# Attention with two feed-forward layers on one core: every full key tile enters the values' product as float32, v comes in one load and a copy, and the maxima's halves are joined ahead of the transpose

## The chip, the core and the metric

The kernel runs on one core of a Trainium2 chip. The time is the device time of one execution in microseconds (us). The kernel before takes 1217.23 us in the median of three runs (1215.57 to 1217.28).

## What is computed

The reference, cut to what matters (4 batches, 8 heads, 576 positions, 64 columns a head; 2304 tokens, 512 columns):

```python
q_rot, k_rot = rotate(q), rotate(k)
scores = (q_rot @ k_rot.T) / sqrt(64)
scores = scores - max(scores, axis=-1)
attn = exp(scores)
attn = attn / (sum(attn, axis=-1) + 1e-09)
x = attn @ v                                   # heads put side by side
x = (sigmoid(x @ w_gate) * (x @ w_val)) @ w_out
h = x @ w_in2
out = where(h > 0, h, exp(min(h, 0)) - 1) @ w_out2
```

## The kernel before

Two stages follow each other. The first is attention over 32 heads (16 pairs), the second is two feed-forward layers over chunks of their weights. The change touches the first alone.

**Tiles.** The 576 keys of a head are four full tiles of 128 and a tail of 64; the 576 queries are two halves of 288. A float32 number x is often held as two parts, a rounded one (hi, type float32r) and the rest (lo = x - hi), so that three float32r products, or fewer, stand for one float32 product.

**Slots and steps.** The program is written out slot by slot, one slot for a head, ten steps in a slot. In step h of slot i, `scores` (L433) issues two matmuls `s` (L459) for tile h // 2 and query half h % 2 of head i, and ScalarE (ACT) takes the exponential; `maxima` (L404) issues one matmul `mt` (L409) for head i + 2, whose negated row maximum VectorE (DVE) takes (L412); `values` (L475) adds one key tile of head i - 1 to its output in PSUM. TensorE (PE) therefore runs s, s, mt and the values' product in every step. Scores use three PSUM banks in turn, the maxima's matmuls three, the values' two.

**An agenda.** Everything else stands in a table, `at(slot, step, function)`: it is issued after the matmuls of that step, and with a half step ahead of the next one's. [...]

- `split_v` (L388): for tiles 0 to 2 of a pair, ACT casts v to a rounded part (VS, L393) and GpSimd (POOL) subtracts (L394); for the tail, L399 and L400 do the same into VT. The agenda has them at steps 1 and 5 of the pair's first slot.
- `scores` for tiles 0 to 2: ACT takes the exponential twice, once into float32 `e` (L462) and once rounded into `ph` (L464); `low_part` (L468) subtracts into `pl` (L471), on DVE for tiles 0 and 2 and the tail, on POOL for tile 1.
- `values` for tiles 0 to 2: three float32r matmuls (L497 to L499). Tile 3 goes as float32: one matmul (L494) of `e` with VF, which the trace shows as two. The tail takes two float32r matmuls (L491, L492).
- Heads 30 and 31 (`LF`, L375) take all five tiles as float32 out of `last_v`.
- `max_all` (L416) joins the two query-half columns of a head's maxima, `max_row` (L420) transposes them on PE (`mr`, L422), ACT copies the row (L424), and a DMA `W<-row` (L426) puts it into the head's operand buffer W, where the head's first scores need it one slot later.
- `rope_ops` (L286) rotates k, q and the tails of a later pair, on POOL in all but the first pair; `split` (L316) transposes them on PE into one of the scores' PSUM banks and makes hi and lo; `move` (L344) copies them into W with three DMAs (`W<-hl`, L358 to L360).
- `inverse` (L519) sends the sums through DRAM and back (`d<-SUM`, `r<-d`, `d<-r`, `rb<-d`), and POOL multiplies (`normalized`, L539).

**Queue.** Every DMA is issued by SyncE (SP), in the order of the agenda. For one pair that is: loads of k and q two pairs ahead (step 0 of an even slot) and of their tails in every other even slot (step 0), the rows (step 1.5 of every slot), the moves (steps 1 and 9 of an odd slot), the sums, v for four heads as three loads of one tile each (step 6 of slots 3, 7, ...), its tails, and VF (step 1 of an odd slot), 256 bytes a row.

**End of the stage.** From slot 29, step 4, the first chunk of the weights is split on DVE, seven instructions for a piece (L124 to L137), between the attention's last steps.

Of the kernel before, what the change touches and what calls it, by code (L numbers as in the profile page):

```python
# [19 lines left out]
def attention_moe_moe_kernel(  # L20
# [40 lines left out]
    NS, NF = len(SP), len(FP)  # L61
# [108 lines left out]
    with ExitStack() as att:  # L170
# [3 lines left out]
        p_p = att.enter_context(tc.tile_pool(name="p", bufs=2 * NS))  # L174
# [39 lines left out]
        def tiles_of_v(b, h, n, t):  # L214
            return v[b, h : h + n, 0:SM, :].rearrange("h (p t) d -> p h t d", t=ST)[:, :, t]

        def load_vf(pr):
            for n in range(NF):
                nc.sync.dma_start(out=VF[pr % 2][:, :, n, 0:D], in_=tiles_of_v(*divmod(2 * pr, H), 2, FP[n]))

# [29 lines left out]
        VF = [const.tile([P, 2, NF, 2 * D], F32, name=f"VF{par}") for par in range(2)]  # L250
        VS = [const.tile([P, 2, NS, 3 * D], F32R, name=f"VS{par}") for par in range(2)]
# [15 lines left out]
        def constants_v(par):  # L267
            nc.gpsimd.memset(VF[par][:, :, :, D : 2 * D], 1.0)
            nc.gpsimd.memset(VS[par][:, :, :, 2 * D : 3 * D].bitcast(F32), 1.0)
# [16 lines left out]
        def rope_ops(pr, which, eng):  # L286


            hd = D // 2
# [26 lines left out]
        def split(pr, which, half):  # L316

            if (pr, which) == (pr, "k") and half == 0:
                if pr == 1:

                    parts[pr] = [p_p.tile([P, S], F32R, tag=tag, name=f"hl1_{n}") for n, tag in enumerate(("ph", "pl", "ph", "pl"))]
                else:
                    parts[pr] = hl_p.tile([P, 4, S], F32R, tag="hl", name=f"hl{pr}")
# [96 lines left out]
        def max_row(i):  # L420
# [7 lines left out]
                in_=row.bitcast(F32),  # L428
            )

        probs = {}

        def scores(i, h):  # L433

# [404 lines left out]
```

## Time and profile before

| | |
|---|---|
| median of three runs | 1217.23 us |
| the profiled execution | 1214.78 us, its span 1213.0 us |
| PE | 1163.2 us busy (96%) |
| DVE | 995.6 us (82%) |
| POOL | 689.2 us (57%) |
| ACT | 499.4 us (41%) |
| mean granted TensorE clock | 0.990 |

Busy time is what an engine spent in instructions; matmuls are pipelined, so that a busy PE need not be a full one. What a change in one stage is worth is read from that stage alone: the attention's heads, its end, and the feed-forward layers have different limits. A wait is put down to what came last of the things waited for.

### The profile page before, as it was taken

The page shows a single profiled execution, that of the slowest core. Times are in us where ns is not written, and L with a number is a line of the kernel's source. Part 1 is how long each engine was busy: PE and PEld are TensorE (multiplying, and loading weights), DVE is VectorE, ACT ScalarE, POOL GpSimd, SP SyncE. Part 2 cuts the span into 40 slices and gives each one's busy share as a digit, 9 for nine tenths or more (in the row PEclk, how much of TensorE's full clock was granted, in tenths as well). Part 3 has the DMA queues.
Part 4 walks back from the last instruction along what each step waited for, and adds up shares of the span by engine and source line. Part 5 has one row for each costly group of instructions (what it writes and reads, how often), then busy time and mean ns, then how long its engine had stood idle before and what let it go on. Part 6 is the DMA issues. An engine that isn't in the chain of part 4 may idle for free.

```text
span 1213.0 us, 17583 instructions
## 1 busy us (share of the span) xinstructions
PE 1163.2 (96%) x5956; PEld 983.2 (81%) x5956; DVE 995.6 (82%) x2024; ACT 499.4 (41%) x1251; POOL 689.2 (57%) x731
## 2 busy tenths in 40 slices
PE   5898999999889999999999999999999999999998
PEld 4787888887857888888888888888888887888887
DVE  8888887887798987867777676778999999999844
ACT  3777777877744532122222222344422222222221
POOL 8977888887355555443444344666554545545421
PEclk9999999999999999999999999999999999999999
DMA  7676666755523121111111111101111111110004
GB/s 186 138 154 140 137 151 140 158 131 128 137 73 97 36 70 53 51 37 36 53 39 49 52 36 35 35 20 51 53 35 53 35 52 36 53 36 18 1 35 122
DMA packets 71146, 89.53 MB, mean 74 GB/s; under 512 B 35920, under 2 KB 44400, under 8 KB 71056
## 3 DMA queue, kind: packets, MB, share of 16 engines
q1 hardware_dynamic: 71056, 88.41, 28.4%
q8 instruction: 47, 0.77, 0.3%
q14 instruction: 43, 0.35, 0.1%
HBM read 56.01 MB, written 4.87 MB: 50 GB/s over the span
## 4 chain that ended last, share of the span: by engine, by line
PE 58%; DVE 9%; ACT 1%; issue 0%
PE h L680 12%; PE h L681 12%; PE h L682 12%; PE o L680 8%; PE o L681 8%; PE o L682 8%; DVE z L763 2%; DVE g L706 1%; DVE g L705 1%; DVE ca L130 1%; DVE cm L137 1%; DVE cm L127 1%; DVE ce L124 1%; DVE ce L133 1%; DVE cm L125 1%
## 5 line engine op out<-in xcount | busy, mean ns | idle before, releaser
L712 POOL TENSOR_TENSOR gl<-g,gh 128x512 fp32r<-128x512 f32 (+1 forms) x140 | 168.6, 1204 | 326.2 <-ACT gh L711 260.4
L711 ACT CAST gh<-g 128x512 fp32r<-128x512 f32 (+1 forms) x140 | 81.2, 580 | 306.6 <-DVE g L706 172.0
L459 PE MATMUL s<-W 128*128 128x288 f32 (+1 forms) x640 | 164.2, 339 | 22.9 <-DMA W<-row 9.6
L680 PE MATMUL h<-xh,wh 128*128 128x512 f32 (+1 forms) x480 | 177.3, 369 | 1.7 <-ACT xh L665 1.3
L681 PE MATMUL h<-xl,wh 128*128 128x512 f32 (+1 forms) x480 | 177.5, 370 | 1.0 <-DVE xl L666 1.0
L682 PE MATMUL h<-xh,wl 128*128 128x512 f32 (+1 forms) x480 | 177.1, 369 | 0.0
L138 POOL TENSOR_TENSOR ca<-ca,wh 128x256 f32<-128x256 f32 x136 | 113.8, 837 | 94.6 <-DVE cm L134 89.0
L412 DVE TENSOR_REDUCE MX<-mt 128x1 f32<-128x288 f32 (+1 forms) x320 | 132.6, 444 | 23.4 <-PE mt L409 22.0
L462 ACT ACTIVATE e<-s 128x288 f32<-128x288 f32 (+1 forms) x320 | 127.7, 411 | 50.1 <-PE s L459 10.8
L135 ACT CAST wh<-ca 128x256 fp32r<-128x256 f32 x136 | 55.3, 407 | 215.9 <-DVE ca L130 215.9
L459 PEld LDWEIGHTS s<-W 128*128 128x128 f32 (+1 forms) x640 | 101.1, 185 | 48.2 <-ACT ph L464 13.8
L140 POOL TENSOR_TENSOR wl<-ca,cm 128x256 fp32r<-128x256 f32 x136 | 113.0, 831 | 18.5 <-DVE cm L137 11.4
L681 PE MATMUL h<-yl,wh 128*128 128x512 f32 (+1 forms) x320 | 117.7, 368 | 0.0
L682 PE MATMUL h<-yh,wl 128*128 128x512 f32 (+1 forms) x320 | 117.7, 368 | 0.0
L680 PE MATMUL h<-yh,wh 128*128 128x512 f32 (+1 forms) x320 | 117.7, 368 | 0.0
L680 PE MATMUL o<-wh,gh 128*128 128x512 f32 x288 | 112.8, 392 | 1.6 <-DVE z L763 1.2
L681 PE MATMUL o<-wl,gh 128*128 128x512 f32 x288 | 112.2, 390 | 0.0
L682 PE MATMUL o<-wh,gl 128*128 128x512 f32 x288 | 112.1, 389 | 0.0
L701 DVE TENSOR_TENSOR g<-h,g 128x512 f32<-128x512 f32 (+1 forms) x60 | 38.2, 637 | 88.6 <-PE h L682 85.8
L409 PE MATMUL mt<-W 128*128 128x288 f32 (+1 forms) x320 | 100.5, 322 | 7.5 <-DVE MX L412 4.5
L680 PEld LDWEIGHTS h<-xh,wh 128*128 128x128 f32 x480 | 90.9, 189 | 17.9 <-ACT xh L665 1.7
L681 PEld LDWEIGHTS h<-xl,wh 128*128 128x128 f32 x480 | 90.8, 189 | 16.4 <-DVE xl L666 1.5
(116 smaller groups left out, 2875.2 us busy)
## 6 DMA issues: line engine op xcount, KB each, us to landing
W<-hl SPq DMA_DIRECT2D x89, 288.0 KB
raw<-in_moe_w_out_dram SPq DMA_DIRECT2D x28, 512.0 KB
raw<-in_moe_w_in_dram SPq DMA_DIRECT2D x16, 512.0 KB
raw<-in_moe_w_gate_dram SPq DMA_DIRECT2D x12, 512.0 KB
raw<-in_moe_w_val_dram SPq DMA_DIRECT2D x12, 512.0 KB
rb<-d SPq DMA_DIRECT2D x32, 144.0 KB
k<-in_k_dram SPq DMA_DIRECT2D x16, 256.0 KB
q<-in_q_dram SPq DMA_DIRECT2D x16, 256.0 KB
```

The costliest lines, as they stand in the source:

```text
L135: nc.scalar.copy(h, a)
L138: nc.gpsimd.tensor_tensor(out=a, in0=a, in1=h.bitcast(F32), op=ALU.subtract)
L140: nc.gpsimd.tensor_tensor(out=l, in0=a, in1=mf, op=ALU.add)
L409: nc.tensor.matmul(m[0:n, 0:HS], lhsT=operand(i, "Q1", t * P, n), rhs=operand(i, "K1", a * HS, HS), start=True, stop=True)
L412: nc.vector.tensor_reduce(out=MX[i % 3][0:n, a, t : t + 1], in_=m[0:n, 0:HS], axis=AX.X, op=ALU.max, negate=True)
L459: nc.tensor.matmul(s, lhsT=operand(i, st, t * P, n), rhs=operand(i, mv, a * HS, HS), start=st == "K1", stop=st == "K2")
L462: nc.scalar.activation(e[:, c], s, AF.Exp)
L680: nc.tensor.matmul(ps, lhsT=ah, rhs=bh, start=j == 0, stop=False)
L681: nc.tensor.matmul(ps, lhsT=ah, rhs=bl, start=False, stop=False)
L682: nc.tensor.matmul(ps, lhsT=al, rhs=bh, start=False, stop=j == n - 1)
L711: nc.scalar.copy(hi, g)
L712: nc.gpsimd.tensor_tensor(out=lo, in0=g, in1=hi.bitcast(F32), op=ALU.subtract)
```

## The change

All four full key tiles go the way of tile 3 before: one exponential into float32 `e`, no rounded part and no low part, one float32 matmul with VF. VF holds all four tiles; v comes in one load of 1 KB pieces for four heads, and POOL copies it into VF, two slots after the load. VS, `load_vf`, `load_last` and the special way of heads 30 and 31 are gone; those two heads now take the tail's way of the others. `max_all` stands at step 0.5, ahead of `max_row` at 1.5 (before: at 2, behind it, so that the row held the first half's maxima alone). The rotation is three instructions instead of four. Pair 1 is moved with three DMAs for each head as the other pairs are. Loads of k and q go from step 0 to 3, tails from 0 to 4, v from slot 4g - 1, step 6 to slot 4g - 2, step 8, the first move of a pair from step 11 to 12, and `split_v` from steps 1 and 5 to 5 and 7. PSUM tiles keep one bank each.

```diff
-    KINDS = ("vector","gpsimd","vector",None)
-    FP = [t for t, kind in enumerate(KINDS) if kind is None]
-    SP = [t for t, kind in enumerate(KINDS) if kind is not None]
...
-        p_p = att.enter_context(tc.tile_pool(name="p", bufs=2 * NS))
+        p_p = att.enter_context(tc.tile_pool(name="p", bufs=2))
...
         def load_v(g):
-            b, h = divmod(4 * g, H)
-            t = raws["v", g] = v_p.tile([P, 4, NS, D], F32, tag="v", name=f"v{g}")
-            for n in range(NS):
-                nc.sync.dma_start(out=t[:, :, n], in_=tiles_of_v(b, h, 4, SP[n]))
+            load("v", 4 * g, 4, v_p)
             load_tails("vv", g, v_p)
...
-        VF = [const.tile([P, 2, NF, 2 * D], F32, name=f"VF{par}") for par in range(2)]
-        VS = [const.tile([P, 2, NS, 3 * D], F32R, name=f"VS{par}") for par in range(2)]
+        VF = [const.tile([P, 2, ST, 2 * D], F32, name=f"VF{par}") for par in range(2)]
...
-            for a in range(2):
-                lo, hi = slice(a * hd, (a + 1) * hd), slice((1 - a) * hd, (2 - a) * hd)
-                tt(out=sv[..., lo], in0=x[..., hi], in1=sin[..., lo], op=ALU.mult)
-                yield
+            axes = "p n" if which == "t" else "p h t"
+            two = lambda y: y.rearrange(f"{axes} (two d) -> {axes} two d", two=2)
+            tt(out=two(sv), in0=two(x)[..., ::-1, :], in1=two(sin), op=ALU.mult)
+            yield
...
             if piece == 0:
-                vs = VS[par]
-                nc.scalar.copy(vs[..., D : 2 * D], x)
-                nc.gpsimd.tensor_tensor(
-                    out=vs[..., 0:D], in0=x, in1=vs[..., D : 2 * D].bitcast(F32), op=ALU.subtract
-                )
+                nc.gpsimd.tensor_copy(VF[par][..., 0:D], x)
...
+                if t == ST:
+                    tail[i] = e_p.tile([P, S], F32, tag="e", name=f"e{i}_{t}")[TL:P]
+                    probs[i, t] = p_p.tile([P, S], F32R, tag="pt", name=f"pt{i}")
                 else:
+                    probs[i, t] = e_p.tile([P, S], F32, tag="ef", name=f"e{i}_{t}", bufs=2 * ST)
...
             nc.scalar.activation(e[:, c], s, AF.Exp)
-            if hi is not None:
-                nc.scalar.activation(hi[:, c], s, AF.Exp)
+            if t == ST:
+                nc.scalar.activation(probs[i, t][TL:P, c], s, AF.Exp)
...
-            elif hi is None:
-                nc.tensor.matmul(out_ps, lhsT=VF[par][:, ab, FP.index(t)], rhs=e[:, c], start=t == 0, stop=False)
-            else:
-                vs = VS[par][:, ab, SP.index(t)]
-                nc.tensor.matmul(out_ps, lhsT=vs[:, D : 3 * D], rhs=lo[:, c], start=t == 0, stop=False)
-                nc.tensor.matmul(out_ps[0:D], lhsT=vs[:, 0:D], rhs=hi[:, c], start=False, stop=False)
-                nc.tensor.matmul(out_ps, lhsT=vs[:, D : 3 * D], rhs=hi[:, c], start=False, stop=False)
+            else:
+                nc.tensor.matmul(out_ps, lhsT=VF[par][:, ab, t], rhs=e, start=t == 0, stop=False)
...
-            at(*((i - 2, 9) if i == 0 else (i - 1, 2)), max_all, i)
+            at(*((i - 2, 9) if i == 0 else (i - 1, 0.5)), max_all, i)
...
-                at(s0 - 4, 15 if pr == 2 else 11, move, pr, 0)
+                at(s0 - 4, 15 if pr == 2 else 12, move, pr, 0)
                 at(s0 - 4, 19, move, pr, 1)
             for piece in range(2 if pr > 0 else 0):
-                at(s0, (1, 5)[piece], split_v, pr, piece)
-            if pr > 1:
-                at(s0 - 1, 1, load_vf, pr)
+                at(s0, (5, 7)[piece], split_v, pr, piece)
         for pr in range(2, NPAIR):
-            slot, step = {3: (-1, 9), 4: (1, 0)}.get(pr, (2 * pr - 8, 0))
+            slot, step = {3: (-1, 9), 4: (1, 3)}.get(pr, (2 * pr - 8, 3))
...
-            at(*((1, 0) if g == 2 else (4 * g - 8, 0)), load_tails, "qk", g, raw_p)
-            at(4 * g - 1, 6, load_v, g)
+            at(*((1, 4) if g == 2 else (4 * g - 8, 4)), load_tails, "qk", g, raw_p)
+            at(4 * g - 2, 8, load_v, g)
...
-        at(*(29, 0), load_last)
```

On SP, the DMAs from slot 19 to slot 20 stood like this before (r8, d2_8 and rb8 are the sums of pair 8, W11 is the operand buffer of head 23, v5 and vv5 are v for heads 20 to 23, k28, q28 and qk7 the loads of a later pair, and row21 is the row of head 21):

```order
L530 DMA r8_3551<-d2_8_3550 128x9
L211 DMA v5_3626<-in_v_dram 128x4x64 x3
L202 DMA vv5_3630<-in_v_dram 64x4x64 x2
L358 DMA W11_158<-hl11_3438 64x1152
L359 DMA W11_158<-hl11_3438 64x2x576
L360 DMA W11_158<-hl11_3438 64x1152
L533 DMA d2_8_3550<-r8_3551 128x9
L192 DMA k28_3687<-in_k_dram 128x2x256
L192 DMA q28_3689<-in_q_dram 128x2x256
L202 DMA qk7_3691<-in_q_dram 64x4x64
L202 DMA qk7_3691<-in_k_dram 64x4x64
L426 DMA W01_156<-row21_3714 1x5x128
```

and now, from v for the same heads on:

```order
L186 DMA v20_2906<-in_v_dram 128x4x256
L196 DMA vv5_2908<-in_v_dram 64x4x64 x2
L451 DMA d2_8_2964<-SUM_88 2x576
L372 DMA W00_153<-row20_2969 1x5x128
L322 DMA W10_155<-hl11_2863 64x1152
L323 DMA W10_155<-hl11_2863 64x2x576
L324 DMA W10_155<-hl11_2863 64x1152
L453 DMA r8_2965<-d2_8_2964 128x9
L322 DMA W11_156<-hl11_2863 64x1152
L323 DMA W11_156<-hl11_2863 64x2x576
L324 DMA W11_156<-hl11_2863 64x1152
L456 DMA d2_8_2964<-r8_2965 128x9
```

Row 21 is the next DMA behind these, and k28 and q28 stand behind it. So between the sums and the row of head 21 the loads of v, of k and q and of their tails are gone, and the row of head 20 and the sums stand ahead of a pair's first move, which they followed before.

On ACT, the first steps of slot 28 stood like this before (e28 and ph28 are the two exponentials, VS0 the rounded v of heads 28 and 29, v7 its load):

```order
L462 ACTIVATE e28_0_4984<-s28_1_5001 128x288
L464 ACTIVATE ph28_0_4985<-s28_1_5001 128x288
L393 CAST VS0_161<-v7_4939 128x6x64
L424 CAST row29_5016<-mr29_5014 5x128
L462 ACTIVATE e28_1_5019<-s28_2_5022 128x288
L464 ACTIVATE ph28_1_5020<-s28_2_5022 128x288
```

and now:

```order
L397 ACTIVATE e28_0_4136<-s28_0_4137 128x288
L397 ACTIVATE e28_0_4136<-s28_1_4149 128x288
L370 CAST row29_4159<-mr29_4157 5x128
L397 ACTIVATE e28_1_4162<-s28_2_4163 128x288
L397 ACTIVATE e28_1_4162<-s28_3_4171 128x288
```

The second exponential of each step and the cast that reads v7 have left ACT; the copy that reads v7 now stands on POOL.

On DVE, at the turn from slot 18 to slot 19 (mt20_9 is the last matmul of head 20's maxima, MX2 where they stand, pt18 the tail's low part), it was:

```order
L412 TENSOR_REDUCE MX2_167<-mt20_9_3496 64x1
L412 TENSOR_REDUCE MX0_165<-mt21_0_3517 128x1
L513 COPY u8_3269<-pv17_1_3431 64x288
L342 TENSOR_TENSOR hl11_3438<-Tq11_256_3525,hl11_3438 128x320
L471 TENSOR_TENSOR pt18_3474<-e18_4_3473,pt18_3474 64x576
L412 TENSOR_REDUCE MX0_165<-mt21_1_3537 128x1
L412 TENSOR_REDUCE MX0_165<-mt21_2_3566 128x1
L418 TENSOR_TENSOR MX2_167<-MX2_167 128x5
L471 TENSOR_TENSOR pl19_0_3511<-e19_0_3509,ph19_0_3510 128x576
```

and it is now:

```order
L358 TENSOR_REDUCE MX2_163<-mt20_9_2922 64x1
L358 TENSOR_REDUCE MX0_161<-mt21_0_2939 128x1
L437 COPY u8_2729<-pv17_1_2859 64x288
L364 TENSOR_TENSOR MX2_163<-MX2_163 128x5
L314 TENSOR_TENSOR hl11_2863<-Tq11_256_2946,hl11_2863 128x320
L404 TENSOR_TENSOR pt18_2896<-e18_4_2895,pt18_2896 64x576
L358 TENSOR_REDUCE MX0_161<-mt21_1_2957 128x1
L358 TENSOR_REDUCE MX0_161<-mt21_2_2977 128x1
```

The join of the halves has moved up four places, and PE's transpose mr20, two steps into the slot, now needs it; the low part pl19 is gone.

## Rows read from the trace of the kernel before

**Rows 1.** Stages: us, busy PE, PEld, DVE, ACT, POOL, clock, DMA share, GB/s.

```profile
25.90:65.80 39.90, 36.44 (x231) 31.48 (x230) 34.51 (x71) 30.83 (x95) 37.20 (x39) 1.00 0.60 134
65.80:246.80 181.00, 167.94 (x1061) 146.74 (x1059) 147.61 (x318) 138.99 (x414) 149.37 (x154) 0.96 0.66 146
246.80:328.20 81.40, 74.52 (x488) 66.61 (x486) 66.07 (x145) 62.34 (x187) 53.51 (x54) 0.98 0.61 141
328.20:366.00 37.80, 30.37 (x155) 23.02 (x152) 36.67 (x81) 20.91 (x60) 22.39 (x25) 0.95 0.23 63
366.00:1213.00 847.00, 840.30 (x3983) 705.76 (x3983) 688.99 (x1364) 238.81 (x486) 405.13 (x420) 1.00 0.15 46
```

**Rows 2.** The same stretches, transposes mr of the maxima alone, one a head.

```profile
25.90:65.80 39.90, 1.23 (x4) 0.35 (x4) 1.00 (x4) 1.00 0.60 134
65.80:246.80 181.00, 5.07 (x17) 1.59 (x17) 4.32 (x17) 0.96 0.66 146
246.80:328.20 81.40, 2.17 (x8) 0.69 (x8) 2.03 (x8) 0.98 0.61 141
```

**Rows 3.** Timeline of PE, two maxima transposes: start, us, engine, line, operation, tiles.

```profile
246.84 0.27 PE L422 MATMUL mr<-ident,MX 128*5 128x128 f32 x1
...
254.81 0.27 PE L422 MATMUL mr<-ident,MX 128*5 128x128 f32 x1
```

**Rows 4.** Timeline of PE, two steps of slot 19, and transposes of slot 18.

```profile
216.69 0.38 PE L330 MATMUL Tk<-ident,rk 128*128 128x128 f32 x2
216.96 0.54 PE L459 MATMUL s<-W 128*128 128x288 f32 x2
...
219.03 0.38 PE L330 MATMUL Tk<-ident,rk 128*128 128x128 f32 x2
...
219.54 0.47 PE L459 MATMUL s<-W 128*64 128x288 f32 x2
...
224.17 0.29 PE L409 MATMUL mt<-W 128*128 128x288 f32 x1
...
224.96 0.30 PE L409 MATMUL mt<-W 128*128 128x288 f32 x1
225.10 0.65 PE L494 MATMUL pv<-e,VF 128*128 128x288 f32 x2
...
225.85 0.29 PE L409 MATMUL mt<-W 128*128 128x288 f32 x1
```

**Rows 5.** Timeline of SP, from a pair's first move to head 21's row.

```profile
223.59 0.49 SPq L358 DMA_DIRECT2D W<-hl  x1
...
230.38 1.48 SPq L211 DMA_DIRECT2D v<-in_v_dram  x3
...
237.27 1.29 SPq L192 DMA_DIRECT2D k<-in_k_dram  x1
...
240.56 0.77 SPq L426 DMA_DIRECT2D W<-row  x1
```

**Rows 6.** Timeline of PE, the first scores of slot 21, idle before in brackets.

```profile
243.20 0.61 PE L459 MATMUL s<-W 128*128 128x288 f32 x1 [2.02 <-DMA W<-row]
```

**Rows 7.** Timelines of ACT and of PE in slot 28.

```profile
319.76 0.51 ACT L393 CAST VS<-v 128x384 fp32r<-128x384 f32 x1 [4.65 <-DMA v<-in_v_dram]
...
321.08 0.54 PE L459 MATMUL s<-W 128*128 128x288 f32 x2 [3.30 <-ACT ph L464]
```

**Rows 8.** Groups by line: busy us in all, mean ns, idle before.

```profile
L464 ACT ACTIVATE ph<-s 128x288 fp32r<-128x288 f32 x180 | 73.0, 406 | 0.0
L471 DVE TENSOR_TENSOR pl<-e,ph 128x576 fp32r<-128x576 f32 x60 | 60.5, 1009 | 0.0
L471 POOL TENSOR_TENSOR pl<-e,ph 128x576 fp32r<-128x576 f32 x30 | 43.5, 1450 | 6.9 <-ACT ph L464 6.9
```

**Rows 9.** Stages, columns of rows 1, around a pair's first move.

```profile
224.00:229.00 5.00, 5.00 (x37) 4.66 (x36) 4.70 (x12) 3.78 (x13) 4.92 (x7) 1.00 0.85 180
229.00:230.40 1.40, 1.40 (x11) 1.24 (x10) 1.40 (x3) 1.26 (x5) 1.40 (x2) 1.00 0.04 11
```

More of the change, by code (lines that the diff above doesn't have):

```diff
@@ L316, in split @@
         def split(pr, which, half):
-            if (pr, which) == (pr, "k") and half == 0:
-                if pr == 1:
-                    parts[pr] = [p_p.tile([P, S], F32R, tag=tag, name=f"hl1_{n}") for n, tag in enumerate(("ph", "pl", "ph", "pl"))]
-                else:
-                    parts[pr] = hl_p.tile([P, 4, S], F32R, tag="hl", name=f"hl{pr}")
+            if which == "k" and half == 0:
+                parts[pr] = hl_p.tile([P, 4, S], F32R, tag="hl", name=f"hl{pr}")
             r, rt = rot[pr, which], rot[pr, "t"]
@@ L326, in split @@
             c0, c1 = ((0, HM), (HM, S))[half]
-            T = ps_qk.tile([P, 512], F32, tag="qk", name=f"T{which}{pr}_{c0}")
-            for c in range(c0, c1, P):
-                if c < SM:
-                    nc.tensor.transpose(T[:, c - c0 : c - c0 + P], r[:, c // P].rearrange("p h d -> p (h d)"), ident)
-                else:
-                    nc.tensor.transpose(
-                        T[:, c - c0 : c1 - c0],
-                        rt[o : o + TL].rearrange("p h d -> p (h d)"),
-                        ident[o : o + TL, o : o + TL],
-                    )
-            hl = parts[pr]
-            n = 0 if which == "k" else 2
-            hi, lo = (hl[m][:, c0:c1] if pr == 1 else hl[:, m, c0:c1] for m in (n, n + 1))
-            T = T[:, 0 : c1 - c0]
+            T = ps_qk.tile([P, 512], F32, tag="qk", name=f"T{which}{pr}_{c0}")[:, 0 : c1 - c0]
+            for c in range(c0, min(c1, SM), P):
+                nc.tensor.transpose(T[:, c - c0 : c - c0 + P], r[:, c // P].rearrange("p h d -> p (h d)"), ident)
+            if half:
+                nc.tensor.transpose(
+                    T[:, SM - c0 :], rt[o : o + TL].rearrange("p h d -> p (h d)"), ident[o : o + TL, o : o + TL]
+                )
+            hi, lo = (parts[pr][:, n, c0:c1] for n in ((0, 1) if which == "k" else (2, 3)))
             nc.scalar.copy(hi, T)
@@ L348, in move @@
             slots = W[pr % NPAR][ab][:, 0 : 4 * S].bitcast(F32).rearrange("p (j s) -> p j s", j=4)
-            if pr == 1:
-                hk, lk, hq, lq = (x.bitcast(F32) for x in parts[pr])
-                nc.sync.dma_start(out=slots[z, 1], in_=lk[r])
-                nc.sync.dma_start(out=slots[r, 0:2], in_=hk[r].unsqueeze(1).to_broadcast([D, 2, S]))
-                nc.sync.dma_start(out=slots[z, 2], in_=hq[r])
-                nc.sync.dma_start(out=slots[r, 2], in_=hq[r])
-                nc.sync.dma_start(out=slots[r, 3], in_=lq[r])
-                return
             src = parts[pr].bitcast(F32)
@@ L372, in copies @@
                     nc.vector.tensor_copy(w[0:D, j * S : (j + 1) * S], hl[:, j])
-        LF = 30
-        last_v = {}
-        def load_last():
-            last_v[0] = hl_p.tile([P, NHEAD - LF, ST + 1, 2 * D], F32, tag="hl", name="last_v")
-            nc.gpsimd.memset(last_v[0][:, :, :, D : 2 * D], 1.0)
-            b, h = divmod(LF, H)
-            for t in range(ST):
-                nc.sync.dma_start(out=last_v[0][:, :, t, 0:D], in_=tiles_of_v(b, h, NHEAD - LF, t))
-            nc.sync.dma_start(
-                out=last_v[0][0:TL, :, ST, 0:D], in_=v[b, h : h + NHEAD - LF, SM:S, :].rearrange("h p d -> p h d")
-            )
         def split_v(pr, piece):
@@ L429, in max_row @@
             )
-        probs = {}
+        probs, tail = {}, {}
         def scores(i, h):
```

53 lines of the change are left out of this document (10 added, 43 removed).

## The prediction

> **What bounds the kernel now.** The profiled execution took 1214.78 us, 2.45 us less than the median of the three runs; sums are made against it, and 2.45 is added at the end. About 2.4 us, 0.2%, is what a measurement of this kernel can tell from no change.
>
> I began with the stages [rows 1]. From 366 us on PE is busy 840.3 of 847 us: the feed-forward layers are PE's, and the change does not touch them. From 328.2 to 366.0, the end of attention, DVE is busy 36.67 of 37.8 us: that stage is DVE's, because the first weights are split there. Between lies the attention proper, where in the long stretch PE, DVE and POOL are each busy over 80% of the time, and the shares do not say who sets the pace. The count of the maxima transposes gives the heads: 4, 17 and 8 in 39.9, 181.0 and 81.4 us [rows 2], so 9.98, 10.65 and 10.18 us a head.
>
> The step length says how far PE is from its own limit. Step 2 of slot 19, with three float32r products, lasts 224.96 - 224.17 = 0.79 us from mt to mt; it holds six matmuls, 0.13 us each [rows 4]. Ten steps without a transpose of k or q last 254.81 - 246.84 = 7.97 us [rows 3], which is such steps end to end. The transposes of a pair add, from Tk to the next s, 216.96 - 216.69 = 0.27 us for a first half and 219.54 - 219.03 = 0.51 us for a second [rows 4], and q's the same, 1.56 us in all. So PE needs 2 x 7.97 + 1.56 = 17.5 us for a pair, 8.75 a head. The 25 heads of the second and third stretch take 262.4 us, where PE needs 219: **43 us of waiting**.
>
> Two of the waits can be read. SP issues v, then moves and sums, then k, q and tails, without a pause from 230.38 until the row of head 21 gets its turn at 240.56 [rows 5]; that head's first scores wait 2.02 us for the row [rows 6]. Such a hole also costs clock: the granted clock is 0.96 over the 181 us [rows 1], 7 us lost, and the loads of k and q with tails come every fourth head, four times in these 17 heads, so 1.8 us each. And in slot 28 the cast of v stands between exponentials on ACT and waits 4.65 us for v; PE's scores then wait 3.30 us for an exponential [rows 7]. The rest are short waits behind ACT and DVE, which in a step of 0.79 us have two exponentials (0.406 us for the rounded one) and every second step a low part of 1.009 us beside a maximum [rows 8].
>
> **The change, part by part.**
>
> *PE's products.* A step with one float32 product lasts 225.85 - 224.96 = 0.89 us [rows 4], 0.10 longer than one with three float32r products. Six of ten steps change, in heads 0 to 29: 180 steps, **+18 us of PE's work**. Per pair: 18.7 us instead of 17.5. It counts in full only if PE waits for nothing. The row is what the sum uses. The Trainium skill (FP8 and Floating Point Precision, TensorE Precision Notes) has a rule that speaks against the change: a true float32 product makes four passes through the array. Worked out as an estimate, at 0.13 us a pass, that rule gives 0.53 us against 0.40 for three products, +24 us in all, and by it the forecast would come out 6 us higher; the row has 0.03 us less a step, and the measurement decides.
>
> *Removed from ACT and DVE.* 180 exponentials (73.0 us) and the low parts of tiles 0 and 2 (60.5 us) go [rows 8], 2.4 and 2.0 us a head. ACT then has about 0.45 us in a step and DVE one maximum and what is spread out, both under PE's 0.89. So their short waits go. What covers the rest of DVE's work is PE's step; without that cover a pair's transposes, whose subtractions meet a copy and a maximum in one step, would show, a few tenths a pair.
>
> *POOL.* The low parts of tile 1 (43.5 us, 1.45 each [rows 8]) and the subtraction for VS go; 16 copies of v come. A copy is not in the trace: between nothing and 1.45 us, since it reads one operand where that row reads two. I take 1. POOL has 31.6 us idle in the 181 [rows 1] and gains more, so it costs nothing; were POOL behind, the next head's values would wait. One rotation instruction takes the place of two half ones, likewise.
>
> *DMA and SP.* v is one load instead of three and no VF loads are left, and none stands in front of a row any more: between a pair's sums and the odd head's row there are only that pair's second moves. The hole of [rows 6] should go in whole, 2.0 + 1.8 us every fourth head while k and q are loaded. The load of v waits for POOL's copy out of its single buffer, with the row and the first moves behind it in the queue; the copy is at step 5, the load at 8, and a row has seven steps to arrive, so this is hidden.
>
> *The first move of a pair* goes one step later and behind the row and the sums. Before: issued from 223.59, DMA busy until 229.0, then quiet [rows 5, 9], and slot 20 begins eight steps after 224.17, near 230.5: 1.5 us to spare. Now it starts 0.89 (a step) plus 0.77 (the row's issue) plus some tenths later, about 2 us, in a slot that is 0.6 us longer. Between nothing and 1 us of PE waiting a pair.
>
> *The joined maxima.* mr now waits for DVE's join, after two maxima and a copy; PE brings two steps, 1.8 us, DVE about 1.5. Between nothing and 0.5 us a head; I take a tenth.
>
> *v's cast off ACT.* The wait of [rows 7] goes: the copy is on POOL, and v is loaded one slot and eight steps ahead of it.
>
> *The end.* DVE still splits the weights at its own pace. Two low parts of head 29 go, two tails' low parts (heads 30 and 31) come: 0, between -2 and +2 us. *The first four heads:* half the exponentials and fewer moves, but POOL's rotations (37.2 of 39.9 us busy) stay: -2 us, between -6 and 0.
>
> **The sum.** All of this leaves PE's 18.7 us a pair plus what is still waited for, r. From the moves, the join and the subtractions I take r = 0.4, so 19.1 a pair, 9.55 a head. 17 heads: 162.4, -18.6. 8 heads: 76.4, -5.0. First heads -2, end 0: **-25.6 us**. 1214.78 - 25.6 = 1189.2, and with the 2.45 of the median: **1192 us**. In general the change is 12.5 (18.7 + r) - 262.4 - 2 = 12.5 r - 30.7.
>
> **Rivals.**
>
> *Half of the waiting stays.* DVE and POOL still have over 80% of a slot at times, and the end of a slot has the join, a move and the sums' round trip together. r = 1.5: -12 us, **1205 us**. For it: even a stage with fewer loads, 246.8 to 328.2, lost 1.4 us a head [rows 1]. Against: those losses stand beside work that is now gone.
>
> *Slower: the first maxima of every even head wait for the late move.* Place: mt of an even slot's step 0, PE idle at each pair. The point from which it decides is r = 2.45 us. A wait like that of [rows 6], 2.0 us with 1.8 us of clock, would give r = 3.8: +17 us, **1234 us**. For it: the move has next to nothing to spare in my reckoning. Against: to lose 2 us it would have to land 2 us later than reckoned, while DMA is busy 0.66 of the time and loses requests.
>
> *PE without a gap.* r = 0, first heads -6, end -2: -37 us, **1181 us**.
>
> *It does nothing:* were the pace set by DMA, a head would stay at 10.5 us. At a DMA share of 0.66 that is hardly so; it is part of the chance of no difference.
>
> **How the numbers follow.** Forecast (1182 to 1200) 0.62; half of it stays (1200 to 1214) 0.19; PE without a gap 0.06; late moves and the like, slower, 0.10; no difference 0.03. So faster 0.87, same 0.03, slower 0.10. The range runs from the bounds of the first heads and the end with r = 0, 1180 us, to r = 2.0, 1212 us; beyond stand the slower rival and no difference.
>
> **What would show it.** The heads of the second stretch should take 9.3 to 9.8 us each, PE's steps 0.89 us without brackets; `W<-row` should be gone from PE's waits, ACT and DVE be busy 60 to 75% there, the clock near 1. The end of attention should last its 37 to 39 us with DVE full, and the layers behind it 847 us. `W<-hl` or the join as a releaser of PE with over 1 us a pair would show the second or third case; a float32 step well over 0.89 us would show the price wrong.

## The result and the profile after

The changed kernel takes 1203.42 us (median of 4 runs, 1202.41 to 1204.34) where the kernel before took 1216.40 beside it (4 runs, 1215.40 to 1217.28): a ratio of 0.9892, with a 95% interval of 0.9877 to 0.9907. It is faster by 13 us. The forecast was 1192, 25 us faster than the 1217.23 known then; 1203.4 lies in the range of 1180 to 1212, but in the part that had a chance of 0.19 (1200 to 1214, the rival "half of the waiting stays", 1205), not in the part that had 0.62. The profiled execution took 1202.41 us with a span of 1200.6.

The stages, cut at the same maxima transposes as in [rows 1], with the same columns:

```profile
26.90:69.50 42.60, 37.50 (x210) 31.52 (x211) 26.70 (x64) 25.10 (x67) 28.46 (x28) 0.92 0.64 151
69.50:239.10 169.60, 161.72 (x959) 135.30 (x958) 124.29 (x282) 113.17 (x301) 97.41 (x109) 1.00 0.66 151
239.10:317.70 78.60, 74.40 (x440) 62.53 (x439) 54.99 (x130) 51.17 (x136) 32.41 (x37) 1.00 0.61 141
317.70:354.00 36.30, 27.46 (x144) 21.27 (x143) 34.55 (x80) 20.50 (x56) 18.89 (x23) 1.00 0.24 68
354.00:1200.60 846.60, 840.11 (x3983) 706.12 (x3983) 688.46 (x1364) 238.54 (x486) 404.90 (x420) 1.00 0.15 46
```

| stretch | before | after | difference | forecast |
|---|---|---|---|---|
| up to the second head's transpose | 25.9 | 26.9 | +1.0 | no term |
| first four heads | 39.9 | 42.6 | +2.7 | -2 |
| 17 heads | 181.0 | 169.6 | -11.4 | -18.6 |
| 8 heads | 81.4 | 78.6 | -2.8 | -5.0 |
| end and feed-forward layers | 884.8 | 882.9 | -1.9 | 0 |

The +1.0 of the first line is no larger than the spread: in the profiled executions of all kernels here that transpose stood between 25.2 and 27.9 us. In the first four heads the granted clock is 0.92, where it was 1.00 [rows 1], which is 3.3 us of full clock. It was at its lower level, 1.2 GHz, from 26.6 to 33.4 us; before it fell, PE was busy 5.89 of 6.80 us (columns as above):

```profile
19.80:26.60 6.80, 5.89 (x25) 4.20 (x24) 5.66 (x15) 2.43 (x7) 6.56 (x13) 1.00 0.45 123
26.60:33.40 6.80, 5.46 (x22) 5.09 (x23) 2.44 (x7) 2.85 (x8) 6.57 (x7) 0.50 0.96 199
```

In the 17 heads DVE, ACT and POOL came down to 73, 67 and 57% of the time, the granted clock rose from 0.96 to 1.00, and PE is busy 95%. What is still waited for is near the pairs' boundaries. These are the waits of PE and of its weight load in the changed kernel (what waited, for what, then us in total, times, longest):

```profile
PE mt L355 <- DMA W<-hl: 14.6, 14, 2.6
...
PE mr L368 <- DVE MX L364: 6.5, 6, 2.4
```

```profile
PEld mr L368 <- DVE MX L364: 12.6, 15, 2.8
```

No wait of PE for the row is left in this list, where the kernel before had [rows 6]. In its place stand the first move of a pair (`W<-hl`) and DVE's join (`MX`, L364): the two terms that the forecast, together with the subtractions, put at 0.4 us a pair.

A boundary at close range, from slot 17 to 18. First the timeline of SP's queue (start, us, what is issued), then of PE, of DVE and of POOL, with the idle time before an instruction in brackets:

```profile
199.73 0.79 SPq L372 DMA_DIRECT2D W<-row  x1
200.62 0.54 SPq L322 DMA_DIRECT2D W<-hl  x1
...
202.72 1.32 SPq L453 DMA_DIRECT2D r<-d  x1
```

```profile
206.86 0.37 PE L355 MATMUL mt<-W 128*128 128x288 f32 x1 [0.62 <-DMA W<-hl]
...
208.63 0.27 PE L368 MATMUL mr<-ident,MX 128*5 128x128 f32 x1
```

```profile
206.93 0.22 DVE L455 RECIPROCAL r<-r 128x9 f32<-128x9 f32 x1 [0.72 <-DMA r<-d]
...
208.01 0.57 DVE L364 TENSOR_TENSOR MX<-MX 128x5 f32<-128x5 f32 x1
208.61 0.75 DVE L404 TENSOR_TENSOR pt<-e,pt 64x576 fp32r<-64x576 f32 x1
```

```profile
206.71 0.62 POOL L342 COPY VF<-v 128x512 f32<-128x512 f32 x1
207.28 1.28 POOL L293 TENSOR_TENSOR rk<-rk,sk 128x512 f32<-128x512 f32 x1
```

The move is issued behind the row at 200.62; the next head's first maxima wait 0.62 us for it at 206.86. The sums' small transfer `r<-d` is issued behind the move, and at 206.93 the reciprocal has held DVE for 0.72 us, with a reduction, a copy and the join behind it in DVE's order. And the join of 128x5 numbers takes 0.57 us: it ends at 208.58, POOL's rotation at 208.56. Three suspects, then, in one place, and a fourth at the start, where the first four heads became slower. The experiments take them one by one.

### The profile page after: what moved, and what is told of

Its sections match the earlier page's. It is cut to its first block, busy times and chain, and to the rows that moved or that the text cites. A ratio compares the mean times of both kernels' runs of the same rounds, so it can differ in the third digit from the quotient of the medians.

```text
span 1200.6 us, 16885 instructions
## 1 busy us (share of the span) xinstructions
PE 1154.1 (96%) x5776; PEld 965.5 (80%) x5776; DVE 951.9 (79%) x1964; ACT 456.0 (38%) x1059; POOL 604.4 (50%) x652
## 4 chain that ended last, share of the span: by engine, by line
PE 71%; DVE 20%; DMA 6%; ACT 1%; issue 1%; SPq 0%; DVEq 0%
PE h L598 11%; PE h L599 11%; PE h L600 11%; PE o L598 7%; PE o L599 7%; PE o L600 7%; PE pv L423 7%; DMA W<-hl 5%; PE s L394 5%; DVE z L681 3%; PE mt L355 3%; DVE ca L124 2%; DVE g L624 2%; DVE g L623 2%; DVE cm L121 2%; DVE cm L131 1%
## 5 line engine op out<-in xcount | busy, mean ns | idle before, releaser
L394 PE MATMUL s<-W 128*128 128x288 f32 (+1 forms) x640 | 178.8, 362 | 1.8 <-ACT e L397 1.2
L358 DVE TENSOR_REDUCE MX<-mt 128x1 f32<-128x288 f32 (+1 forms) x320 | 138.8, 450 | 50.2 <-PE mt L355 45.6
L423 PE MATMUL pv<-e,VF 128*128 128x288 f32 x512 | 164.8, 405 | 0.0
L394 PEld LDWEIGHTS s<-W 128*128 128x128 f32 (+1 forms) x640 | 104.6, 181 | 27.3 <-ACT e L397 4.3
L355 PE MATMUL mt<-W 128*128 128x288 f32 (+1 forms) x320 | 97.8, 314 | 18.2 <-DMA W<-hl 14.6
```

The costliest lines, as they stand in the source:

```text
L355: nc.tensor.matmul(m[0:n, 0:HS], lhsT=operand(i, "Q1", t * P, n), rhs=operand(i, "K1", a * HS, HS), start=True, stop=True)
L358: nc.vector.tensor_reduce(out=MX[i % 3][0:n, a, t : t + 1], in_=m[0:n, 0:HS], axis=AX.X, op=ALU.max, negate=True)
L394: nc.tensor.matmul(s, lhsT=operand(i, st, t * P, n), rhs=operand(i, mv, a * HS, HS), start=st == "K1", stop=st == "K2")
L423: nc.tensor.matmul(out_ps, lhsT=VF[par][:, ab, t], rhs=e, start=t == 0, stop=False)
```

## Experiments

Each was timed in five rounds beside the kernel before; ratios are to that kernel. Lines `-` and `+` stand against the changed kernel, except where the kernel before is named.

### 1. The first move one step earlier again

```diff
-                at(s0 - 4, 15 if pr == 2 else 12, move, pr, 0)
+                at(s0 - 4, 15 if pr == 2 else 11, move, pr, 0)
```

> The changed kernel with the first move of a pair one step earlier again, step 11 of its slot instead of 12; all else stays. If the late first move holds the even heads (theory M): PE's wait of mt for W<-hl, 14.6 us in 14 waits, falls below 5 us, the ten steps of odd slots come from 9.4-10.2 us down towards 9.0, and the time falls from 1203.4 to 1193-1199 us. If the join and the reductions behind the reciprocal hold them (theory J): the time stays within 2 us of 1203.4, and the wait turns up as one of mr for MX. If it was only the start (theory S): within 1 us, with the first head's mr at 26.9 us as before. Against the move: the row is now issued behind three moves, so a wait of the scores for the row may come back (0-4 us).

Measured: 1193.72 us, ratio 0.9816 (0.9800 to 0.9833); the changed kernel's interval does not meet it. The waits of PE:

```profile
PE mr L368 <- DVE MX L364: 9.6, 11, 2.3
...
PE mt L355 <- DMA W<-hl: 4.5, 3, 2.8
```

The 14 waits for the move became 3, as theory M has it, and the time fell by 9.7 us. In the profiled execution, the slowest of the five, the 17 heads took 164.51 us and the 8 heads 75.43, together 8.3 less than after. The 17 heads:

```profile
71.89:236.40 164.51, 160.31 (x957) 134.83 (x958) 126.59 (x282) 113.28 (x300) 99.50 (x108) 1.00 0.69 156
```

The start was slower (the second head's transpose at 27.87, the upper end of the spread named above). Meanwhile mr's wait for the join rose from 6.5 us in 6 to 9.6 in 11: a part of what the move had cost was handed on. The same edit shortened DVE's wait for `r<-d`, from 13.1 us to 5.3 in 13 waits each, so that a share of the 9.7 us may be the reciprocal's; no run takes the two apart with the move early.

### 2 and 3. The join behind the transpose, and the reciprocal later

```diff
-            at(*((i - 2, 9) if i == 0 else (i - 1, 0.5)), max_all, i)
+            at(*((i - 2, 9) if i == 0 else (i - 1, 2)), max_all, i)
```

> The changed kernel with the join of the two halves' maxima put behind the transpose; what is transposed and sent as the row is then the first half's maxima alone. Nothing else is left out. Theory J (the join in front of the transpose costs PE): mr's wait for MX, 6.5 us on PE and 12.6 us on the weight load, falls below 3 us together, and the time falls by 4 to 8 us, to 1195-1199. Theory M (PE waits for the move in any case): what mr no longer waits, the next mt does; the time stays within 2 us of 1203.4 and the wait for W<-hl grows by some us.

```diff
-            for part, step in enumerate((0, 4, 8, 12) if late else (1, 5, 9, 13)):
+            for part, step in enumerate((0, 4, 8, 12) if late else (1, 5, 12, 14)):
```

> The changed kernel with the reciprocal of a pair's sums at step 12 instead of 9 and the loads of its result at 14 instead of 13: DVE no longer waits at step 9 for r's transfer behind the move. Theory J in its second form (the reciprocal blocks the reductions and the join): DVE's wait for r<-d, 13.1 us in 13, falls below 2 us, mr's wait for MX falls by half, and the time falls by 3 to 7 us. Theory M: DVE's wait goes as well, but the time stays within 2 us, since mt waits for W<-hl in the same place.

Measured: 1203.28 us for the join (ratio 0.9895, 0.9878 to 0.9911) and 1206.03 for the reciprocal (0.9917, 0.9904 to 0.9930). Neither gained anything. (The second lies 2.6 us above the changed kernel, where theory M allowed 2; their intervals still meet.) In the first the wait for the join shrank to 0.8 us and the wait for the move took its place:

```profile
PE mt L355 <- DMA W<-hl: 15.2, 15, 2.7
```

In the second DVE's wait for `r<-d` was gone, which in the changed kernel is

```profile
DVE r L455 <- DMA r<-d: 13.1, 13, 2.4
```

yet the move's stood as before and mr's for the join rose:

```profile
PE mt L355 <- DMA W<-hl: 14.7, 15, 2.7
PE mr L368 <- DVE MX L364: 8.5, 12, 2.3
```

So theory J falls in both forms as an account of what the forecast missed: while the move is late, the join is hidden behind it. It does not follow that the join is free, which the next experiment shows.

### 4. The join as a reduction, on top of the earlier move

The join was between 0.15 us and 1.27 us long in the traces. In the changed kernel 20 of the 32 joins took more than 0.2 us, and each of these ended 0.02 us after an instruction of POOL that had begun before it. The minimum of two operands is written as a reduction of one operand over the two halves:

```diff
-            nc.vector.tensor_tensor(out=mx[:, 0], in0=mx[:, 0], in1=mx[:, 1], op=ALU.min)
+            nc.vector.tensor_reduce(out=mx[:, 2], in_=mx[:, 0:2].rearrange("p a t -> p t a"), axis=AX.X, op=ALU.min)
...
-                at(s0 - 4, 15 if pr == 2 else 12, move, pr, 0)
+                at(s0 - 4, 15 if pr == 2 else 11, move, pr, 0)
```

(MX gets a third column, and the transpose reads it.)

> The kernel of e1 (first move at step 11) with the join as a reduction of one operand over the two halves into a third column, in place of a tensor_tensor minimum of two operands. In the traces so far the join of 128x5 numbers takes 0.15-0.17 us while POOL is idle, and up to 1.27 us where POOL is in an instruction, ending within 0.05 us of POOL's end. Theory P (DVE's two-operand operation is held by POOL's running one): the reduction is not held, takes 0.2-0.3 us everywhere, PE's wait of mr for MX falls from 9.6 us in 11 to under 3, the ten steps of odd slots come to 8.6-8.9 us, and the time falls from 1193.7 to 1189-1191.5 us. Rival (the join is late because the reductions and the copy ahead of it are): its duration falls or not, but mr still waits over 7 us, and the time is 1192.5-1195.

Measured: 1188.64 us, ratio 0.9779 (0.9764 to 0.9794), which does not meet experiment 1's interval. The group of the join by line (busy us in all, mean ns, idle before), first of experiment 1 and then of this one:

```profile
L364 DVE TENSOR_TENSOR MX<-MX 128x5 f32<-128x5 f32 x32 | 16.2, 508 | 0.5
```

```profile
L364 DVE TENSOR_REDUCE MX<-MX 128x5 f32<-128x10 f32 x32 | 5.0, 155 | 0.5
```

And one join of each kind beside the same instruction of POOL, a rotation of k. Timelines of DVE and POOL in experiment 1:

```profile
186.32 1.15 DVE L364 TENSOR_TENSOR MX<-MX 128x5 f32<-128x5 f32 x1
```

```profile
186.18 1.27 POOL L291 TENSOR_TENSOR rk<-k,tab 128x512 f32<-128x512 f32 x1
```

and in this one:

```profile
199.65 0.15 DVE L364 TENSOR_REDUCE MX<-MX 128x5 f32<-128x10 f32 x1
```

```profile
199.62 1.28 POOL L291 TENSOR_TENSOR rk<-k,tab 128x512 f32<-128x512 f32 x1
```

The first join ends at 187.47, POOL's instruction at 187.45; the second is done after 0.15 us with POOL's instruction still running for more than a microsecond. All 32 reductions take 0.14 to 0.17 us. PE's wait of mr for MX fell from 9.6 us to 2.5, and the 17 heads became PE's:

```profile
68.95:228.63 159.68, 159.31 (x959) 135.23 (x957) 121.75 (x282) 113.25 (x300) 101.11 (x108) 1.00 0.71 162
```

PE is busy 159.31 of 159.68 us. From mr to mr most slots now last 10.11 and 8.49 us in turn, 18.60 a pair.

### 5. The rotation later instead

```diff
-                        ("k", s0 - 6, (8, 8, 9, 9) if pr == 3 else (1,3,6,8)),
+                        ("k", s0 - 6, (8, 8, 9, 9) if pr == 3 else (2,4,6,8)),
...
-                        ("q", *((0, (0, 0, 7, 7)) if pr == 2 else (s0 - 5, (1,3,6,8)))),
+                        ("q", *((0, (0, 0, 7, 7)) if pr == 2 else (s0 - 5, (2,4,6,8)))),
```

with the first move at step 11 as in experiment 1.

> The kernel of e1 with the first two of a rotation's three instructions on POOL at steps 2 and 4 of their slots instead of 1 and 3, so that the join at step 0.5 meets an idle POOL more often. Theory P (DVE held by POOL): the joins of odd heads are below 0.5 us, mr's wait for MX falls to under 5 us, the time to 1190-1192.5. Rival (POOL has no part in it): 1192.5-1195. Against both: rotations that end later can make the next pair's transposes wait (up to +2 us).

Measured: 1194.30 us, ratio 0.9828 (0.9810 to 0.9845): the same as experiment 1. Theory P's price is missed and the time lies in its rival's range, but what experiment 4 shows of the join speaks against that rival. The joins still took 462 ns in the mean (508 there), since other work of POOL met them in the new place: 7 of the long ones the products with the reciprocals, 6 the copies of v (6 and 3 in experiment 1). mr's wait fell to 6.9 us in 8 only. Moving the one that blocks by a step did not free the path; taking the second operand away did.

### 6. The start: pair 1's move, and the loads ahead of pair 2's

Pair 1 is moved by five transfers per head as in the kernel before:

```diff
+            if pr == 1:
+                hl = parts[pr].bitcast(F32)
+                nc.sync.dma_start(out=slots[z, 1], in_=hl[r, 1])
+                nc.sync.dma_start(out=slots[r, 0:2], in_=hl[r, 0:1].to_broadcast([D, 2, S]))
+                nc.sync.dma_start(out=slots[z, 2], in_=hl[r, 2])
+                nc.sync.dma_start(out=slots[r, 2], in_=hl[r, 2])
+                nc.sync.dma_start(out=slots[r, 3], in_=hl[r, 3])
+                return
```

> The changed kernel with pair 1 moved by five transfers per head, as in the kernel before, instead of three; all other pairs stay. Theory S (the coarse transfers of pair 1 must wait for its last split and cost the start): the first transfer is issued about 2 us earlier, the half clock between 26.6 and 33.4 us goes, the first four heads take 40-41 us instead of 42.6, and the time falls by 2 to 4 us, to 1199.5-1201.5. If the start is held by something else (POOL's rotations, the loads): within 1 us of 1203.4.

Measured: 1200.68 us, ratio 0.9877 (0.9862 to 0.9893); this interval and the changed kernel's overlap, so that alone it is not told from it. The first of the four slots fell from 10.87 to 9.25 us, but the next rose from 12.19 to 13.51, and the four took 42.8 us, not the 40 to 41 expected, at a granted clock of 0.93. What had been won was waited for again one head later, at slot 2. There SP's timeline of the changed kernel shows why:

```profile
39.21 0.38 SPq L186 DMA_DIRECT2D k<-in_k_dram  x1
...
41.66 0.55 SPq L322 DMA_DIRECT2D W<-hl  x1
```

```profile
48.35 0.37 PE L355 MATMUL mt<-W 128*128 128x288 f32 x1 [2.64 <-DMA W<-hl]
```

The loads of pair 4's k, q and tails, which the change put three and four steps later, now stand right ahead of pair 2's first move, and the head's first maxima wait 2.64 us. So the last version puts these loads back to steps 0 of slot 1 and takes all the other repairs with it:

```diff
-            slot, step = {3: (-1, 9), 4: (1, 3)}.get(pr, (2 * pr - 8, 3))
+            slot, step = {3: (-1, 9), 4: (1, 0)}.get(pr, (2 * pr - 8, 3))
...
-            at(*((1, 4) if g == 2 else (4 * g - 8, 4)), load_tails, "qk", g, raw_p)
+            at(*((1, 0) if g == 2 else (4 * g - 8, 4)), load_tails, "qk", g, raw_p)
```

> The changed kernel with its four losses undone together: first move at step 11, join as a reduction of one operand, pair 1 moved by five transfers, and pair 4's k, q and tails loaded at step 0 of slot 1 instead of 3 and 4, ahead of pair 2's first move. If the losses are those named and add up: the first four heads 40-41 us instead of 43.3, the rest as in e8 (159.7 and 76.0 us); time 1184-1187. If the start is held by something else: within 1.5 us of e8, 1187-1190.

Measured: 1184.66 us, ratio 0.9746 (0.9733 to 0.9760), below experiment 4's interval and the lowest median of all versions here (its interval meets those of experiment 8). Its stages:

```profile
25.25:64.31 39.06, 36.84 (x210) 30.76 (x210) 25.75 (x64) 25.36 (x68) 29.07 (x31) 0.96 0.65 155
64.31:224.20 159.89, 159.46 (x959) 135.34 (x958) 121.23 (x282) 113.27 (x300) 101.28 (x109) 1.00 0.71 161
224.20:299.40 75.20, 73.71 (x440) 62.37 (x438) 54.16 (x130) 51.39 (x136) 34.28 (x38) 1.00 0.64 147
```

The first four heads take 39.06 us, less than the 39.90 of before, where experiment 4's took 43.25; the rest is as there. This step and the coarse transfers were undone together. One at a time they did much less: 42.8 us with the transfers alone (above), 41.57 with the loads' old order alone (the third kernel of experiment 7).

### 7. Where the gain came from: the order of the loads, or the products

Two kernels made from the one before, and one from the one after. In the first only the loads have their new steps:

```diff
-            slot, step = {3: (-1, 9), 4: (1, 0)}.get(pr, (2 * pr - 8, 0))
+            slot, step = {3: (-1, 9), 4: (1, 3)}.get(pr, (2 * pr - 8, 3))
...
-            at(*((1, 0) if g == 2 else (4 * g - 8, 0)), load_tails, "qk", g, raw_p)
-            at(4 * g - 1, 6, load_v, g)
+            at(*((1, 4) if g == 2 else (4 * g - 8, 4)), load_tails, "qk", g, raw_p)
+            at(4 * g - 2, 8, load_v, g)
```

> The kernel before with the changed steps of the loads alone (k and q at step 3, their tails at 4, v one slot and eight steps earlier than... slot 4g-2, step 8); products, exponentials and the join stay. If the loads ahead of the row were what PE waited for: the 9.6 us of waits for W<-row and their clock go, and the wait for v's cast; time 1196-1204. If ACT and DVE set the pace in the kernel before (theory of the products): the waits change their names, time 1209-1216.

In the second, only tiles 1 to 3 are float32 (and the pool of the parts has four buffers):

```diff
-    KINDS = ("vector","gpsimd","vector",None)
+    KINDS = ("vector",None,None,None)
```

> The kernel before with float32 products for tiles 1 to 3, tile 0 as before; loads, moves and the join stay where they were. If the relief of ACT, DVE and POOL is what gains (theory of the products): steps of 0.89 us without short waits, the waits for the row at 2 us every fourth head stay or grow; time 1200-1208. If the loads' order is what gains: PE's longer products (4 of 10 steps, 0.10 us each, 120 steps, +12 us) come on top of the same holes; time 1216-1228.

The third is the changed kernel with the first edit's lines turned back:

> The changed kernel with the loads' steps of the kernel before: k and q at step 0, tails at 0, v (one load of four heads) at slot 4g-1, step 6. Theory O (with four tiles as float32 PE is the bound, and the two gains, the loads' order and the relief of the engines, are not both to be had): the holes for the row come back every fourth head, but the first four heads fall from 42.6 to about 40 us, as in the kernel before with three tiles as float32 (39.96); time 1200-1207. Rival (the order gains its 20 us with these products too): 1217-1225.

Measured: the loads' order alone 1195.26 us, ratio 0.9833 (0.9816 to 0.9850); three float32 tiles alone 1196.34, 0.9845 (0.9821 to 0.9869); the changed kernel with the old order 1205.52, 0.9917 (0.9904 to 0.9931). Each half gains about 20 us, more than the whole, and a little more than its expectation gave it. With the new products the old order costs about 2 us, no more than the intervals of the two allow for. The 17 heads, first with the order alone, then with the products alone (the 8 heads behind them took 76.34 and 76.20 us):

```profile
67.83:232.47 164.64, 160.82 (x1061) 141.34 (x1059) 147.06 (x317) 137.88 (x414) 150.56 (x154) 1.00 0.71 158
```

```profile
65.18:236.28 171.10, 161.27 (x993) 139.22 (x991) 131.69 (x300) 120.88 (x345) 114.32 (x136) 0.98 0.69 154
```

And PE's wait of the scores for the row, in the kernel before, with the order alone, and in the changed kernel with the old order:

```profile
PE s L459 <- DMA W<-row: 9.6, 5, 2.2
```

```profile
PE s L459 <- DMA W<-row: 1.0, 2, 0.5
```

```profile
PE s L394 <- DMA W<-row: 4.0, 6, 1.4
```

With the loads moved, the waits for the row all but went and the granted clock of the 17 heads rose from 0.96 to 1.00, with ACT, DVE and POOL busy for as many microseconds as before; so those engines' load did not set most of the pace, as the second half of that expectation had it. With the products alone the waits for the row stayed (7.3 us in 5), but most slots without one ran at 9.96 or 8.3 us. What the expectations left out is that both can be true.

How the halves add up can be estimated. The prediction put PE's waiting in the 25 heads at 43 us. At its 17.5 us a pair for PE (12.5 pairs), 22 of them are left with the order alone; at 9.96 + 8.3 us a pair, 19 are left with the products alone. So each half removes 21 to 25 us, together a little more than there is, and the two must overlap. The kernel that comes nearest to both halves, the first of experiment 8, waits 9 us by the same count (160.14 and 76.69 us) and gains 27.9 us, 12 less than the sum of the two. That the changed kernel gains only 13 is due more to its own losses: 18 us, by the ratios, lie between it and the last version of experiment 6.

In the third kernel the waits for the row did come back, but with 1.4 us at the longest, and the granted clock of the 17 heads stayed at 1.00; its first four heads fell to 41.57 us only, not to the 40 expected. Why the old order is so much cheaper there than in the kernel before was not taken apart.

### 8. Fewer float32 products in the repaired order

The kernel before with the loads' order, the join as in experiment 4 and ahead of the transpose, and tile 0 alone (or tiles 0 and 2) as three float32r products:

```diff
-    KINDS = ("vector","gpsimd","vector",None)
+    KINDS = ("vector",None,None,None)
```

> The kernel before with tile 0 alone as three float32r products, tiles 1 to 3 as float32, the changed loads' steps (pair 4's at step 0), the join as a reduction ahead of the transpose, the first move at step 11, pair 1 by five transfers. Theory O (PE is the bound once the holes are gone, so each float32 step costs its 0.10 us in full): pairs of 18.3 us (9.96 + 8.3, the values that e7 shows without holes) against e8's 18.6; 1180-1184. Rival (the products don't matter, PE waits anyway): as e9 or slower, 1185-1190.

```diff
-    KINDS = ("vector","gpsimd","vector",None)
+    KINDS = ("vector",None,"gpsimd",None)
```

> As e11, with tiles 0 and 2 as three float32r products (low parts on DVE and on POOL) and tiles 1 and 3 as float32. Theory O: PE needs 17.9 us a pair, 0.4 less than e11; if DVE, ACT and POOL keep up, 1175-1180. If their short waits are back (e5, three tiles this way, lost 0.9 us a pair with them): pairs of 18.2-18.6 us, 1180-1186.

Measured: 1187.00 us (0.9765, 0.9752 to 0.9779) and 1187.53 (0.9768, 0.9751 to 0.9784). Both miss the 1180 to 1184 and 1175 to 1180 of theory O; the second lies above even its other case. (The 0.9 us a pair in that expectation is 0.9 a head: with the order alone, experiment 7, a pair took 19.3 us where PE needs 17.5.) PE's own need did fall: the slots with transposes take 9.96 and 9.78 us instead of 10.11. The other slots did not follow, mostly 8.6 to 9.2 us with one tile and 8.5 to 9.0 with two, against 8.49 in the last version of experiment 6. PE's wait of mr for the join, of the first kernel and of the second:

```profile
PE mr L422 <- DVE MX L418: 6.1, 11, 1.8
```

```profile
PE mr L422 <- DVE MX L418: 8.0, 14, 2.3
```

In the last version of experiment 6 that wait is 3.5 us in 4. So what the float32 products cost on PE was saved there and lost again in waiting. Whether the low parts cause that waiting is not shown: DVE's reciprocal also waits longer there (10.4 and 12.9 us against 4.9), and these two kernels keep the rotation in four instructions, VF's own loads and the special way of the last two heads.

## Why the prediction was right in sign and missed in size

**The price of a product: right.** A step with a float32 product was put at 0.89 us from the row of tile 3 [rows 4], a pair at 18.7 us. After, two steps of slot 19 on PE's timeline:

```profile
219.13 0.29 PE L355 MATMUL mt<-W 128*128 128x288 f32 x1
...
220.02 0.29 PE L355 MATMUL mt<-W 128*128 128x288 f32 x1
...
220.90 0.29 PE L355 MATMUL mt<-W 128*128 128x288 f32 x1
```

0.89 and 0.88 us; and a pair without waits takes 18.60 (experiment 4). The estimate from four passes (the Trainium skill, FP8 and Floating Point Precision, TensorE Precision Notes) put the step at 0.03 us more; no run here shows that, and the row was the better price.

**That nearly all of the waiting can go: right as to what is possible, not as to what this change does.** Experiment 6 reaches 1184.7 us with PE busy 159.46 of 159.89; that is near the rival "PE without a gap" (1181). The changed kernel keeps a part.

**The step that failed: "From the moves, the join and the subtractions I take r = 0.4".** After, 17 heads in 169.6 us make 19.95 us a pair, so r = 1.25 over the 18.7 of the working; the 8 heads' 78.6 make 19.65, r = 0.95. That is 7.2 and 2.2 of the 13.2 us that the forecast was too low by in the span; the first four heads add 4.7 and the start 1.0, and the end and the layers take 1.9 off. By the runs r consists of:

- *The first move.* The working said that it starts about 2 us later, and of "Between nothing and 1 us" it took at most 0.2 (r = 0.4 less a tenth a head for the join). Experiment 1 shows 164.51 us instead of 169.6: 0.6 us a pair, with a share of the reciprocal's perhaps in it. The bound held; the choice at its low end did not. "1.5 us to spare" was read at a single boundary [rows 5, 9], and what was to spare there was spent.
- *The joined maxima.* "Between nothing and 0.5 us a head; I take a tenth." Experiment 4 against 1, 159.68 against 164.51: 0.57 us a pair, 0.28 a head. The bound held, and the choice was low again. What the working lacked is the join's own length: the trace of before already had a mean of 319 ns for it, at 5 numbers a lane, where it took 0.17 us with POOL idle.
- *The reciprocal behind r<-d* has no term. It held DVE 13.1 us, yet by experiment 3 that costs nothing that could be measured while the move is late; with the move early it was not tried.

What is left with the move early and the join a reduction is r = 0.1. The join in the trace of before, by line as in experiment 4:

```profile
L418 DVE TENSOR_TENSOR MX<-MX 128x5 f32<-128x5 f32 x32 | 10.2, 319 | 1.6 <-PE mr L422 0.7
```

The two terms also hide each other: undoing the join alone gave nothing, undoing the move alone 9.7 us, and then the join 5 more.

**The first four heads: wrong, and outside its bounds.** -2 us, "between -6 and 0", came from "half the exponentials and fewer moves"; measured +2.7, and +1.0 ahead of it where no term stood. (This +1.0 is within the spread of the start.) The step that failed is that only work was counted there, and no queue and no clock: the loads of pair 4 were moved behind a row and right ahead of pair 2's first move, pair 1's fewer, larger transfers each wait for the last split, and 3.3 us of clock went. With both put back, the same products take 39.06 us at a granted clock of 0.96 (experiment 6), where experiment 4 took 43.25. The loads alone can do it: with nothing but their new order, the first four heads of the kernel before take 42.57 us (experiment 7).

**POOL at no cost: half right.** The copy of v takes 0.62 us, within the bounds and below the 1 taken, and POOL has 72 us idle in the 17 heads. But its instructions of up to 1.28 us cost DVE, where the forecast looked at POOL alone: the join waits them out.

**The hole for the row: right.** `W<-row` is gone from PE's waits and the clock went to 1.00 in the long stretch. What that is worth is another matter: the working put such a hole at 3.8 us every fourth head, but undone in the changed kernel the new order is worth about 2 us in all (experiment 7). Right too were the end (-1.5 us, with DVE busy 34.55 of 36.3, a little under the 37 to 39 of the signs) and the layers (846.6). Of the signs to look for, the shares of ACT and DVE came (67 and 73%), the 9.3 to 9.8 us a head did not (9.98). "`W<-hl` or the join as a releaser of PE with over 1 us a pair" came too (14.6 us in 14 waits); it stood for two cases, one of which came.

**The rivals.** "Half of the waiting stays" named the place (the join, a move and the sums' round trip together at the end of a slot) and gave r = 1.5: measured 1.25 and 0.95. The slower rival had the right place, mt of the even slots, and the wrong size: r would have had to be 2.45.

## What to carry to other kernels

When a change removes several waits at once, price what is left at the middle of its bounds, not at the low end: slack read at one boundary is used up by the first transfer that moves, and the waits that come next were hidden until now. Undo the terms in order, since a second wait behind a first one shows nothing when taken away alone. Don't add up gains that were measured one at a time, or take one for its worth in other company: the two halves of this change gain 20 us each, 28 in the kernel nearest to both, and one of them, the loads' order, about 2 in the changed kernel. For each load that is put later, look what stands right behind it in the queue, at the start of the program too, where the slots aren't those of the steady state.

## What the runs showed of the hardware that was not expected

A two-operand DVE operation on 128x5 numbers in SBUF took 0.15 to 0.17 us with POOL idle and up to 1.27 us where it met an instruction of POOL, and it ended with POOL's: all 24 joins of experiment 1 that took more than 0.2 us ended 0.02 us after an instruction of POOL that had begun before them. A one-operand reduction of the same numbers took 0.14 to 0.17 us in all 32 places, with POOL running or not. The Trainium skill (SBUF — State Buffer, SBUF: two separate sides) says that DVE and GpSimd share a pair of ports as an exclusive lock, that a DVE operation with two SBUF inputs needs it against a GpSimd operation that reads SBUF, and that the loser is blocked for the whole of the other's instruction; the traces agree, at 1.15 us against 0.15. It goes the other way as well, in experiment 4: two rows of the timelines of DVE and POOL there,

```profile
199.83 1.68 DVE L404 TENSOR_TENSOR pt<-e,pt 64x576 fp32r<-64x576 f32 x1
```

```profile
200.84 1.15 POOL L342 COPY VF<-v 128x512 f32<-128x512 f32 x1
```

The tail's low part, 0.75 us long at the boundary shown for the changed kernel, takes 1.68 as it begins during POOL's rotation, and POOL's copy of v, 0.62 us there, takes 1.15 as it begins during the low part. Ten of the 16 copies of v in experiment 4 take 1.14 to 1.15 us, each begun during a tail's low part.
